# Positive parts on ScalarE, masked keys from PSUM, half-block masks on VectorE, and a new order in a two-layer attention kernel

## The chip, the cores and the metric

The kernel runs on one core of a Trainium2 chip. Four engines compute: TensorE (PE in the profile; its weight loads are listed apart as PEld), VectorE (DVE), ScalarE (ACT) and GpSimd (POOL). SyncE (SP) issues transfers only. Each engine works through its own queue in order, and they wait for each other by semaphores. The metric is the device time of one execution in microseconds (us); of several runs the median is taken.

## The reference

One sequence of 2048 tokens with 512 features passes through four blocks, each a residual: linear attention (A), sliding-window attention (B), A, B. There are 32 heads of 16 features.

```python
def _A_ref(x, wqkv, wo):            # linear attention
    ...
    phi = lambda t: jnp.where(t > 0, t + 1, jnp.exp(t)) + 1e-6
    pq, pk = phi(q), phi(k)
    kv = jnp.einsum("bhsd,bhse->bhde", pk, v)
    z = jnp.einsum("bhsd->bhd", pk)
    num = jnp.einsum("bhqd,bhde->bhqe", pq, kv)
    den = jnp.einsum("bhqd,bhd->bhq", pq, z)[..., None] + 1e-6
    o = num / den
    ...
def _B_ref(x, wqkv, wo):            # attention over a window of W = 256
    ...
    scores = jnp.einsum("bhqd,bhkd->bhqk", q, k) * (Dh ** -0.5)
    mask = (idx[:, None] - idx[None, :] >= 0) & (idx[:, None] - idx[None, :] < W)
    scores = jnp.where(mask[None, None], scores, -1e9)
    p = _softmax(scores, axis=-1)
    o = jnp.einsum("bhqk,bhkd->bhqd", p, v)
    ...
x = A_x
x = x + _A_ref(_layernorm(x, axis=-1), A_wqkv, A_wo)
x = x + _B_ref(_layernorm(x, axis=-1), B_wqkv, B_wo)
x = x + _A_ref(_layernorm(x, axis=-1), A_wqkv, A_wo)
x = x + _B_ref(_layernorm(x, axis=-1), B_wqkv, B_wo)
```

## The kernel before

**Tiles and phases.** The 2048 tokens are 16 tiles of 128, and x stays on the chip (`xres`). The first linear attention needs a sum over all tokens before any query can be answered, so `graph` (line 929) first runs `a_kv` for all 16 tiles (names beginning "1."): normalization, key and value projection, feature map of the keys, and the sum `kv`. Then comes the first `segment` ("2."): `a_q` and `a_out` per tile finish the first A block, `b_qkv` ("2.b.") makes queries, keys and values of the first B block, and `b_attn` ("2.a.") attends over the window. In the prediction this B block is called layer one and the second one layer two; the title of the change calls the half-block masks those of "layer two", since that block is the second of the four. Keys and values of the second A block ("2k.") follow tile by tile as tiles come out of the first B block, and after their sum the second segment ("3.", "3.b.", "3.a.") does the same as the first and writes the output.

**The feature map.** exp(t) is at most 1 for t <= 0, so phi(t) = max(t, 0) + min(exp(t), 1) + 1e-6. `phi` (lines 677 to 682) takes an exponential on ACT from PSUM (line 679), a minimum and addition on DVE in SBUF (680), and on DVE a maximum with zero of the PSUM bank plus the rest (681). The bank is free after line 681.

**Masked keys.** Scores are taken for four heads at once in four row groups of 32 rows, each of which holds two heads of 16. So that one head's key doesn't meet the other head's query, the keys are stored twice, each time with the rows of one head set to zero: `kbd`. Before, the key bank is copied to `kT` (by ACT or DVE, line 649), and then DVE multiplies `kT` by the two columns of the 0/1 mask `mab` (line 767).

**A tile's attention.** A query tile of 128 tokens needs five blocks of 64 keys that are partly or wholly visible per half: four blocks in "full" scores (`s0` to `s3`, one for each group of eight heads, line 840) and two half blocks (`sH`, lines 803 and 810). In the half blocks, the masked positions get a large negative addend by extra matmuls on PE with the constants `key` and `far` (line 810); then ACT takes the exponentials (830). In the full blocks ACT takes the exponentials first (847) and DVE multiplies two 64-column blocks by the triangles `tri` (859). Value products (871 and 883) sum values and row sums in PSUM, DVE divides (893 and 895), and `wo` (684) transposes the result, projects it and adds it to `xres` (689). Transposes are a DMA of SP (632), or, where the tile is listed in `BYPE`, four PE transposes (639) with a copy out of PSUM (649).

**The order.** Nothing in the code above fixes when an operation runs. `ORDER` (line 304) lists all 2630 operations by the number under which the code creates them. An apostrophe behind a number picks the second engine of those the operation may run on (ACT first, DVE second, for the copies). `schedule` places operations in that order, gives them a free buffer of their ring or a free bank of the eight of PSUM (some operations take two), and `emit` writes each engine's queue in the same order with the needed waits. Costs such as `_act_cost`, `tail` and `kind` are the planner's own figures and don't change what an instruction does. Each engine's queue is therefore the list, with the other engines' entries left out, and what an operation waits for follows from its reads, its writes and from who last held its buffer.

Of the kernel before, what the change touches and what calls it, by code (L numbers as in the profile page):

```python
# [320 lines left out]
909 452 453 454 868 1346 1347 1348 1349 659 660 875 910 911 642 677 661 884 885 455 1350 886 887 662 629 630 631 663 633 634 614 635 888 889 890 891 913 892
893 894 895 678 643 896 897 644 645 914 915 916 968 441 442 443 969 636 444 970 695 905 632 906 907 637 638' 456 942 943 603 908 944 1351 679 457 458 912 898
899 900 680 646 901 1360 1361 1362 1363 917 921 918 647 648 649' 919 696 946 947 948 922 651 652 653 920 926 927 1001 923 1002 1003 713 1338 1339 650 949 1340
924 925 928 929 930 931 1364 938 939 945 1357 1341 1342 940 941 1352 1353 1354 1355 604 1356 654 655 656 975 976 977 1358 1359' 954 955 681 956 957 958 664
950 951 932 933 934 1374 952 953 1365 1375 1376 682 665 666 667 979 1377 980 1378 981 1379 669 670 671 959 960 978 1034 1035 1036 961 962 963 964 1371 982 971
972 973 672 673 1372 1008 1009 1010 674' 1373' 974 1366 1367 987 1368 1369 1370 988 983 639 640 984 965 966 683 684 697 1011 668 698 985 685 986 989 699 700
967 1012 1013 1014 990 992 993 994 991 1067 1068 690 691 995 996 687 1390 1391 1069 1392 1004 1005 692' 657 714 715 686 688 689' 1385 1386 1387' 1041 716 1006
1007 997 998 999 658 717 1042 675 676 1000 1043 1044 1020 1016 1017 1018 1021 1022 1023 1024 1015 705 1019 1045 1046 1393 1394 1047 701 702 703' 1025 1026
1027 1028 1029 1100 1380 1404 1405 704 1101 1102 1381 1395 1406 1407 708 1408 1382 1383 709 706 1037 1048 459 460 710 711 1401 1402 1038 707' 1384 461 462 463
1039 1030 1040 1074 1075 1076 464 465 466 467 468 1053 712 1403' 1054 1055 1056 1057 1049 1050 1051 1031 1032 1033 1078 1079 1080 1052 718 1077 719 720 721'  # L330
722 1058 1133 1134 1135 469 1418 1419 470 1059 1060 1061 1070 1071 471 1072 1062 1063 723 724 472 725' 1073 1107 1108 693 1396 1397 731 732 733 734 735 1109
736 1086 1087 1398 1399 1082 1400 1083 1084 1064 1065 726 727 728 729 1088 1111 1112 1113 1081 1085 1091 1066 1092 1089 1090 1093 1094 1095 1096 1114 1166
# [56 lines left out]
class _Kernel:  # L389
# [238 lines left out]
    def transp(self, n, src, ring, dma=True):  # L628
        s = self.s
        o = ring.buf()  # L630
        if dma:
            s.op(n, {"SP": 1.25}, lambda e, en: e.dma_start_transpose(o.h[:], src.h[:]), reads=[src], writes=[o], new=[o], dma=True)
            return o
# [396 lines left out]
```

## Time and profile before

| | us |
|---|---|
| median of 3 runs | 446.47 |
| lowest and highest run | 443.78, 449.55 |
| the profiled execution, whole | 444.76 |
| its span, first to last instruction | 443.5 |

The mean TensorE clock of the profiled execution was 0.992 of full speed. A line of the profile's groups names source line, engine, operation, output <- input with partitions x elements, a count, then busy us and the mean ns of one, then the idle time before them and what ended it. The view of windows gives an engine's busy time in a stretch of the span, and the chain of waits follows the work that ended last backwards through whatever released it.

### The profile page before, as it was taken

What the parts mean: (1) busy time and instruction counts of PE and PEld (TensorE: products, weight loads), DVE (VectorE), ACT (ScalarE), POOL (GpSimd) and SP (SyncE); (2) the same over time, 40 slices, a digit from 0 to 9 for tenths busy, and PEclk for the clock granted to TensorE, in tenths of its full rate; (3) what the DMA queues carried; (4) which work ended last, traced back from release to release, by engine and by line L of the source; (5) the groups of instructions that cost most, each with busy time, mean ns of one, the idle gap of its engine ahead of it and who ended that gap; (6) DMA issues with size and microseconds to landing.
All of it is one profiled execution on the core that took longest, in us unless ns stands there. A gap on an engine that the chain in (4) does not pass through costs nothing.

```text
span 443.5 us, 19469 instructions
## 1 busy us (share of the span) xinstructions
PE 397.8 (90%) x8641; PEld 283.1 (64%) x8725; DVE 356.4 (80%) x947; ACT 362.4 (82%) x466; POOL 119.3 (27%) x248
## 2 busy tenths in 40 slices
PE   7989798898999998999899989999888898898886
PEld 3535676566666676667586577686666677675554
DVE  7998898899778788789877899899788876665545
ACT  3746236899999999899988545889898999999993
POOL 5428234132123403021304003143153105204100
PEclk9999999999999999999999999999999999999969
DMA  8691334334142213222323002253263212404323
GB/s 271 173 217 29 43 76 72 51 69 62 27 72 42 60 39 56 41 52 51 62 41 60 15 13 51 38 88 68 40 80 72 44 29 59 72 15 71 98 39 98
DMA packets 76660, 29.46 MB, mean 66 GB/s; under 512 B 66336, under 2 KB 74528, under 8 KB 76576
## 3 DMA queue, kind: packets, MB, share of 16 engines
q1 hardware_dynamic: 70896, 22.17, 26.5%
q0 software_dynamic: 4096, 4.46, 4.8%
q10 hardware_dynamic: 1584, 1.57, 1.1%
q8 instruction: 69, 1.13, 1.1%
q14 instruction: 15, 0.12, 0.1%
HBM read 6.29 MB, written 2.10 MB: 19 GB/s over the span
## 4 chain that ended last, share of the span: by engine, by line
ACT 36%; PE 33%; DVE 20%; DMA 7%; issue 2%; POOL 1%; SPq 0%
ACT pF L847 27%; PE ps L658 11%; PE ps L670 7%; ACT pH L830 7%; PE ps L883 5%; DVE stats L618 3%; PE ps L840 3%; PE ps L871 3%; DMA oT<-o 3%; DVE pq L681 3%; DVE o L749 2%; DMA xT<-xn 2%; DVE xres L689 2%; DVE xn L624 1%; PE ps L803 1%
## 5 line engine op out<-in xcount | busy, mean ns | idle before, releaser
L847 ACT ACTIVATE pF<-ps 128x1024 bf16<-128x1024 f32 (+2 forms) x256 | 230.7, 1016 | 9.3 <-PE ps L840 8.3
L622 POOL TENSOR_TENSOR rstd<-mv,const 128x1 f32<-128x1 f32 x64 | 37.0, 581 | 211.5 <-DVE mv L621 211.4
L778 POOL DMA_DIRECT2D vbd<-vt x128 | 67.5, 534 | 80.0 <-DVE vt L649 53.1
L859 DVE TENSOR_TENSOR pF<-pF,const 128x512 bf16<-128x512 bf16 (+1 forms) x128 | 50.1, 399 | 19.3 <-ACT pF L847 18.8
L830 ACT ACTIVATE pH<-ps 128x1024 bf16<-128x1024 f32 (+1 forms) x64 | 59.2, 989 | 6.5 <-PE ps L810 6.2
L679 ACT ACTIVATE E<-ps 128x512 bf16<-128x512 f32 x64 | 38.5, 607 | 29.0 <-PE ps L670 18.5
L883 PE MATMUL ps<-vbd,pF 128*128 128x34 bf16 x1920 | 61.2, 178 | 0.1
L840 PE MATMUL ps<-qT,kbd 32*128 32x128 bf16 x1920 | 50.3, 218 | 9.4 <-ACT pF L847 5.1
L883 PEld LDWEIGHTS ps<-vbd,pF 128*128 128x128 bf16 x1920 | 55.2, 96 | 3.8 <-issue 0.2
L689 DVE TENSOR_TENSOR xres<-ps,xres 128x512 bf16<-128x512 f32 x64 | 43.9, 686 | 13.9 <-PE ps L658 13.2
L840 PEld LDWEIGHTS ps<-qT,kbd 32*128 32x128 bf16 x1920 | 28.8, 93 | 34.2 <-ACT pF L847 18.6
L618 DVE BATCH_NORM_STATS2 stats<-xres 128x6 f32<-128x512 bf16 x64 | 43.8, 686 | 1.2 <-DMA xres<-in_A_x_dram 0.4
L670 PE MATMUL ps<-xT,w_Bk 128*128 128x128 bf16 x512 | 34.1, 219 | 2.9 <-DMA xT<-xn 2.2
L871 PEld LDWEIGHTS ps<-vbd,pH 128*128 128x128 bf16 x960 | 29.9, 96 | 10.6 <-issue 3.3
L871 PE MATMUL ps<-vbd,pH 128*128 128x34 bf16 x960 | 34.8, 179 | 1.2 <-DVE pF L859 0.4
L658 PE MATMUL ps<-w_Bo,oT 128*128 128x512 bf16 x105 | 29.3, 387 | 6.9 <-issue 1.9
L670 PE MATMUL ps<-xT,w_Bq 128*128 128x128 bf16 x512 | 34.9, 219 | 0.1
L670 PEld LDWEIGHTS ps<-xT,w_Bk 128*128 128x128 bf16 x512 | 29.7, 98 | 7.2 <-DMA xT<-xn 3.0
L658 PE MATMUL ps<-w_Av,xTa 128*128 128x512 bf16 x120 | 31.8, 379 | 2.6 <-DMA xTa<-xn 0.8
L670 PE MATMUL ps<-xTa,w_Aq 128*128 128x128 bf16 x512 | 34.0, 219 | 0.0
L658 PE MATMUL ps<-w_Ak,xTa 128*128 128x512 bf16 x119 | 31.3, 380 | 3.0 <-DMA xTa<-xn 1.4
L658 PE MATMUL ps<-w_Ao,oT 128*128 128x512 bf16 x102 | 27.8, 379 | 6.3 <-issue 3.1
(78 smaller groups left out, 563.4 us busy)
## 6 DMA issues: line engine op xcount, KB each, us to landing
vbd<-vt POOLq DMA_DIRECT2D x128, 34.0 KB, 2.0
xres<-in_A_x_dram SPq DMA_DIRECT2D x16, 128.0 KB, 6.1
out_dram<-xres SPq DMA_DIRECT2D x16, 128.0 KB, 2.1
oT<-o SPq DMA_TRANSPOSE x61, 2.7
w_Ak<-in_A_wqkv_dram ACTq DMA_DIRECT2D x1, 512.0 KB, 4.5
w_Av<-in_A_wqkv_dram ACTq DMA_DIRECT2D x1, 512.0 KB, 6.2
w_Aq<-in_A_wqkv_dram ACTq DMA_DIRECT2D x1, 512.0 KB, 8.6
w_Ao<-in_A_wo_dram SPq DMA_DIRECT2D x1, 512.0 KB, 6.7
```

Of the source, the lines that this page charges most:

```text
L618: s.op(n + ".st", {"DVE": 0.595}, lambda e, en: e.bn_stats(a_st, x.h[:]), reads=[x], writes=[st])
L658: i = e.matmul(g.h, xT.h[:, kt, :], w.h[:, kt, :], start=(kt == 0), stop=(kt == 3), skip_group_check=True)
L670: i = e.matmul(g.h[:, f * P:(f + 1) * P], w.h[:, kt, f * P:(f + 1) * P], xT.h[:, kt, :], start=(f == 0 and kt == 0), stop=(kt == 3), skip_ ...
L679: s.op(n + ".e", {"ACT": _act_cost(512)}, lambda e, en: e.activation(E.h[:], g.h, ACT.Exp, bias=0.0), reads=[g], writes=[E])
L689: s.op(n + ".x", {"DVE": _dve_cost(512)}, lambda e, en: e.tensor_tensor(x.h[:], g.h, x.h[:], ALU.add), reads=[g], writes=[x])
L778: return [e.dma_start(vbd.h[64 * a:64 * a + 64, j, a], vt.h[64 * j:64 * j + 64, a]) for j in range(2)]
L830: return e.activation(d, c, ACT.Exp, bias=0.0, scale=DH ** -0.5)
L840: i = e.matmul(ss[r // 2].h[:, r % 2, m * P:m * P + P], kbds[fj[m] // 2].h[32 * r:32 * r + 32, f, fj[m] % 2, :], qT.h[32 * r:32 * r + 32, ...
L847: s.op("e%d%d" % (f, g), {"ACT": _act_cost(2 * (4 - m0) * P)}, lambda e, en, S=ss[g], pb=pb, g=g: e.activation(pb.h[:, 2 * g:2 * g + 2, m0 ...
L859: return e.tensor_tensor(v, v, tr, ALU.mult)
L871: i = e.matmul(U.h[:, c:c + 34], pH.h[:, 4 * r + f, 64 * a:64 * a + P], vbds[j // 2].h[:, j % 2, :, 4 * f + r, :], start=first[0], stop=Tr ...
L883: i = e.matmul(U.h[:, c:c + 34], pFs[f].h[:, r, m * P:m * P + P], vbds[fj[m] // 2].h[:, fj[m] % 2, :, 4 * f + r, :], start=False, stop=Tru ...
```

## The change

1. `PHIA` names three of the four groups of feature maps (keys of the first A block, queries of both; 16 each). There, ACT also takes a Relu of the bank straight into the result, and DVE adds the other part from SBUF.
2. The ring `kT` is gone. Two operations `kb0` and `kb1` a tile write the two halves of `kbd` straight from the PSUM bank, each on ACT (a copy with the mask column as its scale) or on DVE.
3. In the first B block the extra matmuls with `key` and `far` are left out for the half blocks, and two DVE multiplications `mH0` and `mH1` a tile apply the triangles to the exponentials.
4. Tile 0 of the first B block and of the A block before it are transposed on PE (`BYPE`).
5. The last tile of the second B block masks its full blocks by extra matmuls on PE, and ends in `b_end`: four groups of eight heads, each with its own value products, division, transpose, copy and part of the output product; the residual addition and the output transfer run in two halves.
6. `ORDER` is new from its first line to its last, 2732 entries. The copies of queries, values and normalized tiles change engine in places with it.

The diff without the numbers of the order:

```diff
-BYPE = {("x1.", t) for t in range(6)} | {("a2.", 15), ("k2.", 15), ("o3.", 0), ("x3.", 0), ("a3.", 15)}
+PHIA = ("1.k","2.q","3.q")
+HMD = ("2.a.",)
+BYPE = {("x1.", t) for t in range(6)} | {("a2.", 15), ("k2.", 15), ("o3.", 0), ("x3.", 0), ("a3.", 15)} | {("o2.",0),("x2.",0)}
...
-            self.r_kT = self.ring("kT", 3, [P, 4, P])
...
-            s.op(n, {"SP": 1.25}, lambda e, en: e.dma_start_transpose(o.h[:], src.h[:]), reads=[src], writes=[o], new=[o], dma=True)
+            s.op(n, {"SP": 1.25}, lambda e, en: e.dma_start_transpose(o.h[:], src.h[:]), reads=[src], writes=[o], new=[o], dma=True,
+                 tail=1.0 if s.at[0] == "1." else 0.0)
...
+        if s.at[0] + n in PHIA:
+            s.op(n + ".r", {"ACT": _act_cost(512)}, lambda e, en: e.activation(view(o), g.h, ACT.Relu), reads=[g], writes=[o])
+            s.op(n + ".a", {"DVE": 0.335}, lambda e, en: e.tensor_tensor(view(o), view(o), E.h[:], ALU.add), reads=[E], writes=[o])
+            return
...
-        gk = self.proj_feat("k", xT, self.w["Bk"], kT, kbd)
-        self.copy("kc", kT, gk, lambda: (kT.h[:].rearrange("p f c -> p (f c)"), gk.h))
...
-        s.op("kb", {"DVE": 0.525}, kb, reads=[kT, self.mab], writes=[kbd])
+        gk = self.proj_feat("k", xT, self.w["Bk"], kbd)
+        for a in range(2):
+            def kb(e, en, a=a):
+                o = kbd.h[:, :, :, a * 64:a * 64 + 64].rearrange("p f j c -> p (f j) c")
+                g, m = gk.h.rearrange("p (b c) -> p b c", c=64), self.mab.h[:, a:a + 1]
+                return e.activation(o, g, ACT.Copy, scale=m) if en == "ACT" else e.tensor_scalar(o, g, m, None, op0=ALU.mult)
+
+            s.op("kb%d" % a, {"ACT": _act_cost(512), "DVE": _dve_cost(512)}, kb, reads=[gk, self.mab], part=[kbd])
...
-            for a, j in pcs:
+            for a, j in () if s.at[0] in HMD else pcs:
...
-            s.op("eH%d" % g, {"ACT": _act_cost(512 * len(pcs))}, ex, reads=[ss[g]], part=[pH])
+            mH = mH + [_Buf()]
+            s.op("eH%d" % g, {"ACT": _act_cost(512 * len(pcs))}, ex, reads=[ss[g]], writes=[mH[g]], part=[pH])
+        for g in range(2) if s.at[0] in HMD else ():
+            def mkH(e, en, g=g):
+                v = vH(g)
+                tr = self.tri.h[:].unsqueeze(1).to_broadcast([P, 8, 2, 64]) if len(pcs) == 2 else self.tri.h[:, 1:2, :].to_broadcast([P, 8, 64])
+                return e.tensor_tensor(v, v, tr, ALU.mult)
+
+            s.op("mH%d" % g, {"DVE": 0.065 + 0.00054 * 512 * len(pcs)}, mkH, reads=[self.tri, mH[g]], part=[pH])
...
+                for ty, h in ((0, 0), (0, 1), (3, 0), (3, 1)) if split else ():
+                    for r in range(4):
+                        c = ss[r // 2].h[:, r % 2, (64 if ty == 0 else 384) + 32 * h:][:, 0:32]
+                        k = self.key.h[32 * r:32 * r + 32, (0 if ty == 0 else 2) + h].rearrange("p a h c -> p (a h c)")
+                        i = e.matmul(c, k, self.far.h[32 * r:32 * r + 32, ty // 3, 0, :], start=False, stop=True,
+                                     skip_group_check=True, tile_position=(32 * r, 0))
...
+            if split:
+                continue
             s.op("m%d" % f, {"DVE": 0.34 if m0 == 0 else 0.2}, mask, reads=[self.tri], writes=[pb])
+        if split:
+            return self.b_end(t, o, pH, pFs, pcs, fj, vbds, w)
...
+    def b_end(self, t, o, pH, pFs, pcs, fj, vbds, w):
...
+        ys = [self.pG.buf(), self.pG.buf()]
+        for f in range(4):
...
+            s.op("z%dh" % f, {"PE": 0.0255 * 4 * len(pcs)}, pvH, reads=[pH] + [vbds[j // 2] for _, j in pcs], writes=[U], new=[U], kind="sum")
...
+                s.op("z%d%d" % (f, hf), {"PE": 0.0252 * 8}, pvF, reads=[pFs[f]] + [vbds[j // 2] for j in fj], writes=[U], kind="sum")
...
+            s.op("zr%d" % f, {"DVE": 0.12}, lambda e, en, uv=uv, dn=dn: e.reciprocal(dn.h[:, 0:8].unsqueeze(2), uv()[:, :, 16:17]),
+                 reads=[U], writes=[dn], new=[dn], tail=0.11)
+            s.op("zm%d" % f, {"DVE": 0.2}, lambda e, en, f=f, uv=uv, dn=dn: e.tensor_tensor(
+                o.h[:, f * P:f * P + P].rearrange("p (h e) -> p h e", e=DH), uv()[:, :, 0:16],
+                dn.h[:, 0:8].unsqueeze(2).to_broadcast([P, 8, DH]), ALU.mult), reads=[U, dn], part=[o], new=[o] if f == 0 else [])
+            s.op("zT%d" % f, {"PE": 0.1}, lambda e, en, f=f, tp=tp: e.transpose(tp.h.bitcast(BF)[:, 0:P], o.h[:, f * P:f * P + P], self.ident.h[:]),
+                 reads=[o, self.ident], writes=[tp], new=[tp, oT])
...
+            for c in range(2):
+                s.op("zw%d%d" % (f, c), {"PE": 0.12}, lambda e, en, f=f, c=c, oT=oT: e.matmul(
+                    ys[c].h[:, 0:256], oT.h[:, 0, :], w.h[:, f, 256 * c:256 * c + 256], start=(f == 0), stop=(f == 3), skip_group_check=True),
+                    reads=[oT, w], writes=[ys[c]], new=[ys[c]] if f == 0 else [], tail=0.1, kind="tok")
+        for c in range(2):
+            hx = _Buf()
+            s.op("zx%d" % c, {"DVE": _dve_cost(256)}, lambda e, en, c=c: e.tensor_tensor(
+                x.h[:, 256 * c:256 * c + 256], ys[c].h[:, 0:256], x.h[:, 256 * c:256 * c + 256], ALU.add), reads=[x, ys[c]], writes=[hx])
+            d = s.op("zo%d" % c, {"SP": 0.45}, lambda e, en, c=c: e.dma_start(
+                self.out[0, t * P:(t + 1) * P, 256 * c:256 * c + 256], x.h[:, 256 * c:256 * c + 256]), reads=[hx], dma=True)
...
```

More of the change, by code (lines that the diff above doesn't have):

```diff
@@ L321 @@
[L321 to L332, printed above, removed]
@@ new lines @@
+495 1123 1124 761 518 519 757 506 522 496 497 498 1471 1472 1161 1120 1467 1125 758 520 521 1468 1162 1163 762' 759' 1191 1134 1138 1139 1140 1135 1136 1469'
+1165 1166 1155 499 500 501 1164 1137 1143 1141 1142 1222 1473 1167 502 765 766 767 1223 768 1224 1225 1113 1114 1115 1157 1158 1159 1144 769 1145 770 1196
+1197 1198 1146 1147 1462 1463 1464 523 1160 1168 1173 1174 1116 1474 1475 508 1175 1176 1169 1170 1171 1488 1177 771 772 1465 773 774 509 1466 510 1148 511
+1489 512 775 513 778 779 776 1200 1172 1178 1179 1180 746 780 1201 1498 777' 1181 1182 1257 1202 1203 763 1149 1150 1151 1258 1259 1514 1515 1495 1192 1193
@@ L759, in b_qkv @@
         kbd, qT, vbd = self.r_kbd.buf(), self.r_qT.buf(), self.r_vbd.buf()
-        kT, vt = self.r_kT.buf(), self.r_vt.buf()
-        gk = self.proj_feat("k", xT, self.w["Bk"], kT, kbd)
-        self.copy("kc", kT, gk, lambda: (kT.h[:].rearrange("p f c -> p (f c)"), gk.h))
-        def kb(e, en):
-            src = kT.h[:].rearrange("p f (j c) -> p f j c", j=2)
-            for a in range(2):
-                i = e.tensor_scalar(kbd.h[:, :, :, a * 64:a * 64 + 64], src, self.mab.h[:, a:a + 1], None, op0=ALU.mult)
-            return i
-        s.op("kb", {"DVE": 0.525}, kb, reads=[kT, self.mab], writes=[kbd])
+        vt = self.r_vt.buf()
+        gk = self.proj_feat("k", xT, self.w["Bk"], kbd)
[5 more added lines that the diff above has]
+            s.op("kb%d" % a, {"ACT": _act_cost(512), "DVE": _dve_cost(512)}, kb, reads=[gk, self.mab], part=[kbd])
         gq = self.proj_feat("q", xT, self.w["Bq"], qT)
@@ L786, in b_attn @@
         m0 = {0: 3, 1: 1}.get(t, 0)
+        split = last and t == self.T - 1
         fj = [2 * t - 3 + m for m in range(4)]
@@ L813, in mmH @@
             return i
-        ss = scores("sH", pH, [j for _, j in pcs], mmH, 0.24 * len(pcs) + 0.02)
+        ss = scores("sH", pH, [j for _, j in pcs], mmH, 0.24 * len(pcs) + 0.02 - (0.115 * len(pcs) if s.at[0] in HMD else 0))
         def vH(g):
@@ L820, in vH @@
             return d if len(pcs) == 2 else d[:, :, 1, :]
+        mH = []
         for g in range(2):
@@ L842, in mmF @@
                                      skip_group_check=True, tile_position=(32 * r, 0))
+                for ty, h in ((0, 0), (0, 1), (3, 0), (3, 1)) if split else ():
[4 more added lines that the diff above has]
+                                     skip_group_check=True, tile_position=(32 * r, 0))
                 return i
-            ss = scores("s%d" % f, pb, fj[m0:], mmF, 0.025 + 0.056 * (4 - m0))
+            ss = scores("s%d" % f, pb, fj[m0:], mmF, 0.025 + 0.056 * (4 - m0) + (0.09 if split else 0))
             for g in range(2):
@@ L898, in b_attn, with pvH, pvF, uv @@
         self.wo("o", o, w, t, last, dma)
+    def b_end(self, t, o, pH, pFs, pcs, fj, vbds, w):
+        s = self.s
+        x = self.xres[t]
+        ys = [self.pG.buf(), self.pG.buf()]
+        for f in range(4):
+            U, dn, tp, oT = self.pG.buf(), self.r_dn.buf(), self.pG.buf(), self.r_oT.buf()
+            def pvH(e, en, f=f, U=U):
+                for r in range(4):
+                    for a, j in pcs:
+                        i = e.matmul(U.h[:, r * 34:r * 34 + 34], pH.h[:, 4 * r + f, 64 * a:64 * a + P], vbds[j // 2].h[:, j % 2, :, 4 * f + r, :],
+                                     start=(r == 0 and j == pcs[0][1]), stop=True, skip_group_check=True)
+                return i
+            s.op("z%dh" % f, {"PE": 0.0255 * 4 * len(pcs)}, pvH, reads=[pH] + [vbds[j // 2] for _, j in pcs], writes=[U], new=[U], kind="sum")
+            for hf in range(2):
+                def pvF(e, en, f=f, U=U, hf=hf):
+                    for r in (2 * hf, 2 * hf + 1):
+                        for m in range(4):
+                            i = e.matmul(U.h[:, r * 34:r * 34 + 34], pFs[f].h[:, r, m * P:m * P + P], vbds[fj[m] // 2].h[:, fj[m] % 2, :, 4 * f + r, :],
+                                         start=False, stop=True, skip_group_check=True)
+                    return i
+                s.op("z%d%d" % (f, hf), {"PE": 0.0252 * 8}, pvF, reads=[pFs[f]] + [vbds[j // 2] for j in fj], writes=[U], kind="sum")
+            def uv(U=U):
+                return U.h[:, 0:136].rearrange("p (h e) -> p h e", e=17)
+            s.op("zr%d" % f, {"DVE": 0.12}, lambda e, en, uv=uv, dn=dn: e.reciprocal(dn.h[:, 0:8].unsqueeze(2), uv()[:, :, 16:17]),
[5 more added lines that the diff above has]
+                 reads=[o, self.ident], writes=[tp], new=[tp, oT])
+            self.s.op("zc%d" % f, {"ACT": _act_cost(P), "DVE": _dve_cost(P)}, lambda e, en, oT=oT, tp=tp: e.activation(
+                oT.h[:, 0, :], tp.h.bitcast(BF)[:, 0:P], ACT.Copy) if en == "ACT" else e.tensor_copy(oT.h[:, 0, :], tp.h.bitcast(BF)[:, 0:P]),
+                reads=[tp], writes=[oT])
+            for c in range(2):
[8 more added lines that the diff above has]
+                self.out[0, t * P:(t + 1) * P, 256 * c:256 * c + 256], x.h[:, 256 * c:256 * c + 256]), reads=[hx], dma=True)
+            d.final = True
+            d.signals = True
```

70 lines of the change are left out of this document (40 added, 30 removed), and 73 rows, old and new, of the table ORDER.

## The prediction

> **What bounds the kernel now.** First the page's head and its shares of busy time: no engine is a clear bound.
>
> ```profile
> span 443.5 us, 19469 instructions
> PE 397.8 (90%) x8641; PEld 283.1 (64%) x8725; DVE 356.4 (80%) x947; ACT 362.4 (82%) x466; POOL 119.3 (27%) x248
> ACT 36%; PE 33%; DVE 20%; DMA 7%; issue 2%; POOL 1%; SPq 0%
> ```
>
> The third line is the chain that ended last: it passes from ScalarE (ACT) to TensorE (PE) to VectorE (DVE), a third each, so shares over the whole span decide nothing. I therefore cut the span into eight stages and asked the view of windows for the busy time in each. The cuts are the starts of a tile's half-block exponentials (pH, line 830) or the end of a layer's last exponential: layer one tiles 0, 4, 12 and its end, then layer two tiles 0, 4 and its end. Columns: stretch, length, then busy us and instructions of PE, PEld, DVE, ACT, POOL, the clock, DMA.
>
> ```profile
> 0.00:71.40 71.40, 62.59 (x550) 37.22 (x558) 63.21 (x181) 32.64 (x56) 32.79 (x86) 1.00 0.53 131
> 71.40:96.30 24.90, 23.34 (x542) 17.03 (x544) 21.39 (x59) 21.66 (x37) 7.37 (x14) 1.00 0.35 58
> 96.30:183.20 86.90, 79.86 (x2035) 57.51 (x2054) 70.68 (x186) 83.54 (x98) 21.56 (x40) 1.00 0.30 51
> 183.20:241.10 57.90, 53.87 (x1235) 38.06 (x1247) 47.73 (x127) 54.63 (x65) 14.61 (x27) 1.00 0.30 54
> 241.10:273.90 32.80, 31.28 (x449) 23.63 (x451) 30.20 (x80) 16.86 (x31) 2.62 (x5) 1.00 0.11 22
> 273.90:318.30 44.40, 41.17 (x872) 31.16 (x882) 39.58 (x111) 38.05 (x59) 12.51 (x24) 1.00 0.36 61
> 318.30:436.20 117.90, 102.03 (x2907) 76.43 (x2932) 80.59 (x205) 114.39 (x126) 27.82 (x53) 0.97 0.31 59
> 436.20:443.50 7.30, 3.62 (x62) 2.07 (x60) 3.04 (x7) 0.60 (x1) 0.00 (x0) 0.96 0.32 92
> ```
>
> The reader is to see three regimes. Stages 3, 4 and 7 (263 us) belong to ScalarE at 96, 94 and 97% busy. Stages 1 and 5 belong to PE and DVE together, with ScalarE under half busy (32.64 of 71.4 and 16.86 of 32.8). Stages 2 and 6 have all three at 85 to 94%. Work given to ScalarE is cheap in stages 1 and 5 and dear in 3, 4 and 7.
>
> **The prices.** An instruction that queues behind another of its engine costs less than its own duration, so I take the step from one to the next out of the chain and the timeline (start, us, engine, line, count).
>
> ```profile
> 380.07 7.33 ACT pF L847 x8
> 33.46 4.26 PE ps L658 x19
> 250.47 1.08 ACT L649 ACTIVATE vA<-ps 128x512 bf16<-128x512 f32 x2
> 263.12 1.28 DVE L681 SCALAR_TENSOR_TENSOR pq<-ps,E 128x512 bf16<-128x512 f32 x2
> 98.11 0.75 DVE L859 TENSOR_TENSOR pF<-pF,const 128x512 bf16<-128x512 bf16 x2
> 272.21 0.60 DVE L767 TENSOR_SCALAR kbd<-kT,const 128x512 bf16<-128x512 bf16 x2
> 272.73 0.68 DVE L681 SCALAR_TENSOR_TENSOR pq<-ps,E 128x512 bf16<-128x512 f32 x1
> 75.18 0.41 PE L810 MATMUL ps<-const 32*128 32x128 bf16 x16
> 75.53 0.68 PE L670 MATMUL ps<-xT,w_Bk 128*128 128x128 bf16 x9
> L859 DVE TENSOR_TENSOR pF<-pF,const 128x512 bf16<-128x512 bf16 x112 | 45.9, 415 | 17.9 <-ACT pF L847 17.4
> L859 DVE TENSOR_TENSOR pF<-pF,const 128x256 bf16<-128x256 bf16 x16 | 4.2, 286 | 1.4 <-ACT pF L847 1.4
> L679 ACT ACTIVATE E<-ps 128x512 bf16<-128x512 f32 x64 | 38.5, 607 | 29.0 <-PE ps L670 18.5 <-PE ps L658 10.2
> ```
>
> - ACT: 1024 columns 7.33/8 = 0.92 us; 512 columns 1.08 - 0.60 = 0.48.
> - DVE: 512 columns from PSUM 1.28 - 0.68 = 0.60; 512 from SBUF 0.75 - 0.415 = 0.34; a kb pair 272.73 - 272.21 = 0.52. A 1024-column multiply: 415 + 2 x (415 - 286) = 673 ns, less the same 0.08 of overlap, 0.59.
> - PE: 512 columns 4.26/19 = 0.224, so half a projection 0.45; a tile's 16 half-block mask matmuls 75.53 - 75.18 = 0.35 at most.
>
> **Part by part.**
> (1) Positive part. Each of 48 maps gets a Relu on ACT (+48 x 0.48 = 23.0) and its DVE step becomes an SBUF addition in place of a PSUM one (-48 x 0.26 = -12.5). No Relu is in this trace. From below it is an ACT copy out of PSUM (0.48), from above a lone one (0.607); I take 0.48, since it queues behind its own exponential. Exponentials behind it in ScalarE's queue wait those 0.48 longer; the addition waits for it.
> (2) Masked keys. Before: a copy (17 on ACT, 15 on DVE) and a DVE pair. After: 64 half writes from PSUM, 19 on ACT and 45 on DVE by the apostrophes in the new order; eight query copies and other copies move too. ACT: -17 + 19 - 8 + 1 copies, -5 x 0.48. DVE: -15 x 0.60 - 32 x 0.52 + 45 x 0.60 + 7 x 0.60 = +5.6. A half write from PSUM isn't in the trace; between the SBUF half (0.26) and the PSUM copy (0.60) I take 0.60, its source being PSUM. The key bank is now held until both writes end; the two steps in a row become two that may run side by side.
> (3) Layer-one (the code's "2.a.") half-block masks: PE loses at most 16 x 0.35 = 5.6; DVE gains 28 x 0.59 + 4 x 0.34 = 17.9. What waits for them is the first half-block value product, queued behind four score groups; DVE's queue waits behind each mask for its exponential.
> (4) Two more tile-0 transposes on PE with a copy on ACT, in place of SP's DMA, at the start of layer one.
> (5) The tail, below. The dropped key ring frees memory alone; the 1.0 on a transpose is the planner's figure; POOL (27% busy) keeps its statistics and moves in number, and SP issues two transposes less.
>
> In all ACT gains some 22 us and DVE some 10, PE loses about 3: the change adds work. It can only win by where the new order puts it. I named the numbers of both orders, cut them at the same events, and priced the differences. Half projections are h.
>
> 1. Before layer one's first scores: ACT +26 Relus; DVE -10 (23 lighter additions; two fewer residual additions, one fewer statistics, two fewer normalizations); PE -8 h, +2 transposes, -1 numerator pair: -3.0. PE bound: **-3.0**. PE idles 8.8 us here, and DVE, its equal so far, falls to 53; the two transposes leave a queue that shows up as
>
> ```profile
> 47.90 8.65 SPq L632 DMA_TRANSPOSE oT<-o  x5
> 63.26 4.77 DMA xT<-xn
> 5.60 0.60 PE L639 MATMUL ps<-const,xn 128*128 128x128 bf16 x4 [0.32 <-DVE xn L624]
> ```
>
>    1.73 us each in the queue and 4.77 on the chain against 0.60 and a copy of 0.60. I take **-2.0** more; the ends are 0 and -5.
> 2. ACT +0.4, DVE +1.1, PE -1.0: **+0.5**.
> 3. Four Relus and half writes against fewer copies: ACT **+2.0**. DVE takes 17 of the masks, +13.1, and goes from 70.68 to 83.8 of 88.9 us: 81% to 94%.
> 4. Work is brought forward into this stage (two more key maps of the next layer, four of its query maps): ACT **+6.8**, DVE +8.0, PE +5.6.
> 5. In return PE -2.5, DVE -4.0 (ACT +3.5, from 16.86): **-2.5**.
> 6. PE -9.4 (18 h and smaller pieces moved to stages 3 to 5 and 7), DVE -3.5, ACT -3.9. The bound goes from PE's 41.17 to DVE's 36.1: **-5.1**.
> 7. ACT unchanged (112.3 by my prices in both orders), DVE +6.2, PE +8.1 to 110 of 117.9: **0**.
> 8. The tail:
>
> ```profile
> 436.16 0.42 DVE L859 TENSOR_TENSOR pF<-pF,const 128x512 bf16<-128x512 bf16 x1 [0.29 <-ACT pF L847]
> 437.06 0.96 PE L883 MATMUL ps<-vbd,pF 128*128 128x34 bf16 x32
> 438.35 0.42 DVE L895 TENSOR_TENSOR o<-ps,dn 128x256 bf16<-128x256 f32 x1
> 439.26 0.60 ACT L649 ACTIVATE oT<-ps 128x512 bf16<-128x512 bf16 x1 [3.14 <-PE ps L639]
> 440.00 1.02 PE L658 MATMUL ps<-w_Bo,oT 128*128 128x512 bf16 x4 [0.78 <-ACT oT L649]
> 441.07 0.69 DVE L689 TENSOR_TENSOR xres<-ps,xres 128x512 bf16<-128x512 f32 x1 [1.45 <-PE ps L658]
> ```
>
>    With four groups the mask (0.42) and its wait are gone from DVE, the value products are 0.5 in place of 1.0, the copy 0.25 for 0.60, the output product 0.25 for 1.02, and the addition 0.35 a half: 2.9 less, against two additions and two output transfers in turn, 0.8 more. **-2.1.** The masks go to PE, which idles in stage 7.
>
> Beside these, stage 3 brings DVE to 94% beside ACT at 96%. Stage 6 of before shows three near-equal engines: the busiest reaches 41.17/44.4 = 93%, not the 96% of stage 3. Between nothing and stage 3 at that ratio (85.5/0.93 - 88.9 = 3) I take **+1.0**.
> Sum: -3.0 - 2.0 + 0.5 + 2.0 + 6.8 - 2.5 - 5.1 + 0 - 2.1 + 1.0 = **-4.4**, 443.5 to 439.1 us of span. The profiled execution took 444.76 (1.26 beside the span), which makes 440.4; the median of the three runs, 446.47, lies 1.7 above it, so **442 us**.
>
> The Trainium skill ("ScalarE: Activation LUTs", What ACT_TABLE_LOAD costs) gives about 93 ns more to an ACTIVATE for each pointer operand of one value a partition. The new key writes on ACT have one as their scale, and no run here shows it. Fourteen of the 19 stand in stages 2 to 4, 6 and 7, so by the page the sum would be some 1.3 us higher, an estimate.
>
> **Rivals.**
> - *The order closes idle time* (0.34). The busiest engine's idle is 8.2 us in stage 1, 3.2 in stage 6, 3.3 in stage 4 and 3.5 in stage 7. If DVE's relief and the earlier key writes take 3, 3, 1.5 and 2.5 of these beyond my terms, 10 go: 432 us. For it: DVE has 10 us less in stage 1. Against: it has more in 3, 4 and 7.
> - *VectorE's half-block masks take over the path* (0.10, slower). In stages 3 and 4 the DVE queue gets 26 masks, 15.3 us. If each is met by an empty ring of pF, the softmax masks behind it start late, value products hold their PSUM banks, and scores and ACT wait: 442 + 15.3 = 457. It makes the kernel slower by 2% only if 13.3 of the 15.3 lie on the path. Against: DVE has 16.2 and 10.2 us free there.
> - *Relu is the wrong work for ScalarE* (0.03, slower). My sum charges Relus as ScalarE's only where ScalarE bounds; the 35 in stages 1 and 5 ride free. If each delayed its map by its 0.48, 17 us: 459. Against: ACT is idle 39 and 16 us there, and on PSUM sources it steps faster (0.48) than DVE (0.60). The Trainium skill (same page, Rules for kernel authors) says relu belongs on VectorE, up to about three times faster in bf16; the rows just named disagree for a float32 source in PSUM.
> - *Relu costs table loads* (0.01): one each way, 96 of the 1.28 below, 123 us: 565. Against: copies and exponentials alternate all through with two loads in all.
>
> ```profile
> L649 ACT ACT_TABLE_LOAD x1 | 1.3, 1283 | 2.4 <-issue 2.4
> L943 ACT ACT_TABLE_LOAD x1 | 1.3, 1283 | 0.0
> ```
>
> **How the numbers follow.** My forecast has 0.52 and a range of its own of 437 to 450: the ends of stage 1's term, the 3 us of stage 3, a lone Relu's price. A measurement of this kernel tells about 2% from no change (437.5 and 455.4). So faster 0.34 (first rival), same 0.52, slower 0.14 (the others). The range 430 to 453 leaves out the far part of the first rival (0.06) and most of the slower ones (0.12).
>
> **What would show it.** Stage by stage: the first half-block exponential at about 66 us, not 71.4; layer one's last exponential some 5 us later than 241; layer two's tile 0 near 276 to 279; its last exponential near 434; 5.2 us after that. ACT busy near 384, DVE near 366, and the half-block mask line on DVE near 0.6 us a piece. I am wrong if stage 1 isn't shorter, if stage 3 grows by over 6, or if ScalarE waits in stage 7.

## The result and the profile after

The changed kernel takes 432.47 us (median of 4 runs, 430.78 to 433.92) against 445.92 (4 runs) for the kernel before: a ratio of 0.9689, interval 0.9615 to 0.9763. It is 3% faster. The forecast was 442 in a range of 430 to 453, with "no change" as the likeliest case: the range holds the time, the likeliest case was the wrong one, and the time is the one that the rival "the order closes idle time" was priced at (432). How far that rival's mechanism is what happened is taken up below. Of the 9.5 us between 442 and the result, 6.4 lie in the span (439.1 forecast, 432.7 measured); the rest is the step from the profiled execution to the median, +1.7 in the forecast and -1.5 here (433.92 to 432.47). The profiled execution has this span and these shares:

```profile
span 432.7 us, 19801 instructions
PE 408.5 (94%) x8801; PEld 286.6 (66%) x8801; DVE 367.9 (85%) x954; ACT 383.3 (89%) x513; POOL 121.8 (28%) x248
PE 38%; ACT 35%; DVE 17%; DMA 7%; issue 2%; POOL 1%; POOLq 0%; DVEq 0%
```

ACT is busy 383.3 us (forecast 384) and DVE 367.9 (forecast 366): the work did grow by some 21 and 11 us, and the span shrank by 10.8. The view of windows, cut at the same events as before (the pH exponentials of layer one's tiles 0, 4, 12, its last exponential, layer two's tiles 0 and 4, its last exponential), shows where:

```profile
0.00:64.20 64.20, 60.01 (x529) 35.83 (x529) 54.44 (x163) 44.81 (x83) 32.31 (x82) 1.00 0.48 124
64.20:90.90 26.70, 24.20 (x496) 16.37 (x497) 23.92 (x61) 22.21 (x36) 6.85 (x14) 1.00 0.42 80
90.90:181.00 90.10, 85.51 (x2149) 61.82 (x2148) 82.14 (x206) 87.36 (x105) 23.85 (x44) 1.00 0.33 55
181.00:243.00 62.00, 61.23 (x1352) 43.03 (x1350) 55.75 (x144) 60.52 (x77) 15.17 (x28) 1.00 0.30 52
243.00:273.10 30.10, 29.48 (x389) 21.53 (x388) 27.68 (x78) 19.88 (x39) 4.76 (x9) 1.00 0.13 26
273.10:307.80 34.70, 32.68 (x728) 23.43 (x727) 31.12 (x83) 33.01 (x50) 10.86 (x21) 1.00 0.34 62
307.80:427.50 119.70, 112.95 (x3144) 83.35 (x3141) 90.69 (x218) 114.77 (x127) 27.96 (x53) 1.00 0.34 59
427.50:432.70 5.20, 2.42 (x29) 1.25 (x28) 2.14 (x7) 0.76 (x4) 0.00 (x0) 1.00 0.55 180
```

The clock (last column but two) was 1.00 in stages 1 to 6 before and after, and 0.97 and 0.96 before in stages 7 and 8 only, so it doesn't explain what stages 1 to 6 gained or lost.

TensorE's busy time must not be compared between these two profiles as it stands. The profile before has 8641 matmuls for 8725 weight loads: 84 matmuls of the 512-column projections (L658) left no record. The one above has all 8801. The run e5 below is the same changed kernel again, and its profile lacks 84 of them too, as the one before does:

```profile
PE 396.1 (92%) x8717; PEld 286.0 (66%) x8801; DVE 368.0 (85%) x954; ACT 383.3 (89%) x513; POOL 121.8 (28%) x248
0.00:64.04 64.04, 58.16 (x523) 35.18 (x529) 54.47 (x163) 44.82 (x83) 32.36 (x82) 1.00 0.48 125
64.04:90.67 26.63, 23.34 (x491) 16.30 (x497) 23.89 (x61) 22.27 (x37) 6.82 (x14) 1.00 0.45 78
90.67:180.14 89.47, 82.94 (x2128) 61.85 (x2148) 81.97 (x206) 87.26 (x105) 23.86 (x44) 1.00 0.33 55
180.14:242.23 62.09, 59.43 (x1338) 43.01 (x1350) 55.80 (x144) 60.55 (x77) 15.18 (x28) 1.00 0.30 51
242.23:272.26 30.03, 29.14 (x384) 21.55 (x388) 27.66 (x78) 19.82 (x38) 4.71 (x9) 1.00 0.13 26
272.26:307.00 34.74, 32.04 (x722) 23.40 (x727) 31.12 (x83) 33.05 (x49) 10.93 (x21) 1.00 0.34 61
307.00:426.30 119.30, 108.65 (x3117) 83.42 (x3141) 90.93 (x218) 114.82 (x127) 27.96 (x53) 1.00 0.34 59
426.30:431.50 5.20, 2.38 (x29) 1.25 (x28) 2.10 (x7) 0.72 (x3) 0.00 (x0) 1.00 0.55 180
```

TensorE's busy time differs by 12.4 us between the two profiles of the same kernel (408.5 and 396.1), about 0.15 us a record, while the other engines agree within 0.1 us and the stages within 0.7. So the table takes the lengths from both and the rest from e5. For each stage, take its busiest engine out of e5's lines and out of the table before the change; what is left of the stage is time in which even that engine has nothing on record.

| stage | forecast | measured | in e5 | e5: busiest engine's work | its idle time, before -> e5 |
|---|---|---|---|---|---|
| 1 to first exponential | -5.0 | -7.2 | -7.4 | -5.0 | 8.2 -> 5.9 |
| 2 layer one, tiles 0-4 | +0.5 | +1.8 | +1.7 | +0.6 | 1.6 -> 2.7 |
| 3 tiles 4-12 | +3.0 | +3.2 | +2.6 | +3.7 | 3.4 -> 2.2 |
| 4 to its end | +6.8 | +4.1 | +4.2 | +5.9 | 3.3 -> 1.5 |
| 5 between the layers | -2.5 | -2.7 | -2.8 | -2.1 | 1.5 -> 0.9 |
| 6 layer two, tiles 0-4 | -5.1 | -9.7 | -9.7 | -8.1 | 3.2 -> 1.7 |
| 7 to the last exponential | 0 | +1.8 | +1.4 | +0.4 | 3.5 -> 4.5 |
| 8 tail | -2.1 | -2.1 | -2.1 | -1.2 | 3.7 -> 2.8 |

The busiest engines' work fell by 5.9 us in all (415.2 to 409.3) and their idle time by 6.1 (28.3 to 22.2). The forecast had -3.4 for the work and -1.0 for the idle time.

One part did not do what it says. Below, the groups of the changed kernel and of the one before in the stretch 60 to 245 us, which is layer one, and then the DVE multiplication of the changed kernel:

```profile
L818 PE MATMUL ps<-const 32*128 32x128 bf16 x240 | 6.2, 215 | 0.0
L810 PE MATMUL ps<-const 32*128 32x128 bf16 x240 | 6.3, 215 | 0.0
L847 DVE TENSOR_TENSOR pH<-pH,const x32: 391/682/691, 65.6 to 238.2; 128x1024 bf16<-128x1024 bf16 x28, 128x512 bf16<-128x512 bf16 x4
```

All 240 masking matmuls of layer one are still there. The line `for a, j in () if s.at[0] in HMD else pcs` stands in a function that runs when the queues are written out, and by then `s.at` holds the name of the last phase built, "3.a.", whatever tile the function belongs to. The two loops over `mH` and the positive parts ask at the time of building and do work. So the changed kernel masks layer one's half blocks twice, on TensorE before the exponential and on VectorE behind it (a zero times zero). The description in "The change", item 3, is what the code means to do, not what runs.

### The profile page after: what moved, and what is told of

The parts are those of the page before. It is cut to its first block, busy times and chain, and to the rows that moved or that the text cites. A ratio compares the mean times of both kernels' runs of the same rounds, so it can differ in the third digit from the quotient of the medians.

```text
span 432.7 us, 19801 instructions
## 1 busy us (share of the span) xinstructions
PE 408.5 (94%) x8801; PEld 286.6 (66%) x8801; DVE 367.9 (85%) x954; ACT 383.3 (89%) x513; POOL 121.8 (28%) x248
## 4 chain that ended last, share of the span: by engine, by line
PE 38%; ACT 35%; DVE 17%; DMA 7%; issue 2%; POOL 1%; POOLq 0%; DVEq 0%
ACT pF L870 24%; PE ps L663 14%; PE ps L675 7%; ACT pH L839 7%; PE ps L910 4%; DMA oT<-o 4%; PE ps L857 4%; PE ps L898 2%; DVE stats L622 2%; DVE o L758 2%; DVE xres L698 2%; ACT E L684 2%; DVE xn L628 1%; DVE kbd L775 1%; PE ps L720 1%
## 5 line engine op out<-in xcount | busy, mean ns | idle before, releaser
L910 PEld LDWEIGHTS ps<-vbd,pF 128*128 128x128 bf16 x1856 | 54.1, 96 | 5.4
L882 DVE TENSOR_TENSOR pF<-pF,const 128x512 bf16<-128x512 bf16 (+1 forms) x124 | 47.5, 398 | 9.8 <-ACT pF L870 9.5
L698 DVE TENSOR_TENSOR xres<-ps,xres 128x512 bf16<-128x512 f32 x63 | 42.9, 683 | 6.4 <-PE ps L663 6.3
L675 PE MATMUL ps<-xT,w_Bk 128*128 128x128 bf16 x512 | 35.1, 219 | 2.0 <-DMA xT<-xn 1.6
L675 PE MATMUL ps<-xT,w_Bq 128*128 128x128 bf16 x512 | 36.1, 219 | 0.8 <-issue 0.4
L775 DVE TENSOR_SCALAR kbd<-ps,const 128x512 bf16<-128x512 f32 x45 | 31.9, 742 | 5.2 <-PE ps L675 4.7
L663 PE MATMUL ps<-w_Ao,oT 128*128 128x512 bf16 x128 | 33.7, 380 | 1.4 <-DMA oT<-o 0.9
L663 PE MATMUL ps<-w_Ak,xTa 128*128 128x512 bf16 x128 | 33.8, 387 | 1.0 <-ACT xTa L654 0.8
L663 PE MATMUL ps<-w_Av,xTa 128*128 128x512 bf16 x128 | 34.6, 384 | 0.1
L675 PEld LDWEIGHTS ps<-xTa,w_Aq 128*128 128x128 bf16 x512 | 30.4, 98 | 6.4 <-issue 2.0
```

What stands on the lines that cost most here:

```text
L663: i = e.matmul(g.h, xT.h[:, kt, :], w.h[:, kt, :], start=(kt == 0), stop=(kt == 3), skip_group_check=True)
L675: i = e.matmul(g.h[:, f * P:(f + 1) * P], w.h[:, kt, f * P:(f + 1) * P], xT.h[:, kt, :], start=(f == 0 and kt == 0), stop=(kt == 3), skip_ ...
L698: s.op(n + ".x", {"DVE": _dve_cost(512)}, lambda e, en: e.tensor_tensor(x.h[:], g.h, x.h[:], ALU.add), reads=[g], writes=[x])
L882: return e.tensor_tensor(v, v, tr, ALU.mult)
L910: i = e.matmul(U.h[:, c:c + 34], pFs[f].h[:, r, m * P:m * P + P], vbds[fj[m] // 2].h[:, fj[m] % 2, :, 4 * f + r, :], start=False, stop=Tru ...
```

## The experiments

All twelve were timed in five rounds beside the kernel before. They fall into three sittings, on two chips, in which the kernel before took 444.39 us (e1 to e4), 444.87 (e5 to e8) and 446.14 (e9 to e12); so a difference between runs of two sittings is uncertain by a further 1 to 2 us. Orders were rewritten by name: an operation that an edit adds or drops is put in or taken out at the place named below, and where no PSUM banks or ring buffers were free any more, a few entries were moved later. The expectations name three theories: A, the order carries the gain and the parts only make it possible; B, relieving VectorE where ScalarE is idle carries it, whatever the order; C, the order alone carries it.

**The base again.**

> The changed kernel once more, so that the runs beside it have their base on the same chip: 431 to 434 us, ratio near 0.969.

433.16 us (0.974, interval 0.9704 to 0.9777), first half-block exponential at 64.04 us, span 431.5. The differences below are taken against this.

**Layer one's masks.**

```diff
-HMD = ("2.a.",)
+HMD = ()
```

> The changed kernel with layer one's half-block masks back on TensorE, the order otherwise the same. If the masks on VectorE cost what the prediction put in (about 1 us net): 430.5 to 432.5. If TensorE (95 and 99% busy in stages 3 and 4 of the changed kernel) is what bounds there: 16 x 0.35 = 5.6 us of work comes back, 435 to 438.

433.94 us (0.9765, 0.9743 to 0.9786), between the two times on record. Since TensorE's masks had never gone, this run doesn't move them: it only drops the 32 multiplications from VectorE, whose busy time fell to 352.0 us. It tells less than it was meant to, but one thing clearly: 16 us of VectorE's time, most of it in stages 3 and 4 at 91 and 90% busy, were worth nothing (433.94 against 433.16, intervals overlapping). These multiplications don't bound there. TensorE's 95 and 99% in the expectation come from the profile with all records; e5's has 93 and 96%. Whether TensorE without its 240 matmuls would make those stages shorter was not tried, and stays open.

**The positive part.**

```diff
-PHIA = ("1.k","2.q","3.q")
+PHIA = ("2.q","3.q")          # e8; () in e3
...
 order: "<map>.r" taken out, "<map>.a" replaced by "<map>.p" right behind the later of ".r" and ".m"
```

> The changed kernel with the positive part back on VectorE for the 16 key maps of the first stage alone. By the prediction's bound (TensorE, with at most half of its idle time lent by VectorE) 0 to 2 us: 432 to 435. If each map's VectorE time lies on the path of the first stage, as the run without any Relu suggests (10.7 us for 26 maps there): 16/26 of it, 6 to 7 us, 438 to 440, all of it before the first half-block exponential (64.2 us).

436.77 us (0.9823, 0.9793 to 0.9854), 3.6 above the base. The first half-block exponential of this run and of the base:

```profile
68.11 1.08 ACT L839 ACTIVATE pH<-ps 128x512 bf16<-128x512 f32 x2 [0.21 <-PE ps L818]
64.04 1.08 ACT L839 ACTIVATE pH<-ps 128x512 bf16<-128x512 f32 x2 [0.41 <-issue]
```

It starts 4.1 us later, and from there to the end of the span the two run alike (367.2 and 367.5 us). That is 16 x 0.26 = 4.2, the whole price of the heavier VectorE step, and VectorE's busy time in the stage grew by as much (54.47 to 58.72 us). TensorE now waits for that step (L690), 3.0 us in stage 1, where it waited 0.5 for the lighter one of the same maps (L688) in the base:

```profile
PE ps L720 <- DVE pk L690: 1.3, 2, 1.0
PE ps L663 <- DVE pk L690: 0.9, 1, 0.9
PE ps L644 <- DVE pk L690: 0.8, 1, 0.8
```

So in stage 1 VectorE's time lies on the path. The result falls between the two numbers on record: more than the 0 to 2 of a TensorE bound, less than the 6 to 7 read off e3.

> The changed kernel with the 48 positive parts back on VectorE, each maximum as soon as the bank's exponential and minimum are through. If the relief of VectorE is the main cause (A and B alike): 438 us or more, with the first stage (to the first half-block exponential) at 67 us or more where it is 64.2, and layer two's start (tiles 0 to 4, now 34.7 us) longer by 2 or more. If Relu brings nothing: 431 to 434.

470.37 us (1.0583, 1.0556 to 1.061). Both signs that the expectation names for VectorE's relief are there: the first half-block exponential at 74.95 us, and layer two's start 37.7 us long for 34.7. But 37 us is three times the 48 x 0.26 = 12.5 that the Relus took from VectorE. Dozens of other entries of the order had to move to find banks, and ScalarE, with 19 us less to do than in the changed kernel (364.5), waited 34 us for scores. The granted clock was lower too (0.985, base 1.00), and the same 8717 recorded matmuls took 404.2 us for 396.1. This run can't be read as the price of the Relus.

**The masked keys.**

```diff
-            s.op("kb%d" % a, {"ACT": ..., "DVE": ...}, kb, reads=[gk, self.mab], part=[kbd])
+        self.copy("kc", kT, gk, ...)                                  # at the first half write's place
+        s.op("kb", {"DVE": 0.525}, kb, reads=[kT, self.mab], writes=[kbd])   # at the second's; e11: two DVE entries later
```

> The changed kernel with the masked keys in two steps again: a copy of the bank at the place of the first half write (on ScalarE where one of the two halves was there), the DVE pair at the place of the second. By work alone nothing changes (a copy and 0.52 us for two half writes): 431.5 to 434. If the shorter way from the bank to the masked keys is what closed idle time: 437 us or more, most of it in layer two's start (34.7 us) and in layer one's tiles.

451.6 us (1.0157, 1.0117 to 1.0198): 18.4 us more than the base, with the same work (ACT 380.3, DVE 368.6 us busy). VectorE stood 9.0 us before copies that ScalarE hadn't done, which could be my placing; hence the next run.

> The run e6_two_step_keys once more with the DVE pair two VectorE instructions later in the order, so that VectorE seldom stands before a key copy that isn't through (9.0 us of waiting in that run). If that wait made the 18.5 us: 442 or less. If the longer way from bank to masked keys made it, through scores and exponentials that start late: 447 or more.

446.24 us (1.0003, 0.9976 to 1.003). The wait at VectorE's head fell to 4.6 us and the time by 5.4 (the two runs are of two sittings). 13.1 us remain, so neither bound that was on record was met: about a third was the place, the rest the longer way itself or what else the order has fitted to the short one. What carries it is ScalarE's wait for scores. The view of ScalarE's waits, for the run e11 and then for the base:

```profile
ACT pH L843 <- PE ps L822: 12.9, 13, 2.9
ACT pF L874 <- PE ps L861: 12.2, 29, 0.8
...
ACT pF L870 <- PE ps L857: 5.9, 16, 0.8
ACT pH L839 <- PE ps L818: 4.1, 9, 0.8
```

25.1 us against 10.0: 15 us of waiting, 13 us of time. A tile's scores can't start before its keys are masked, and ScalarE, which is the busiest engine in stages 3, 4, 6 and 7, has then nothing to take.

**The tail.**

```diff
-        split = last and t == self.T - 1
+        split = False
```

> The changed kernel with the last tile as before (masks on VectorE, two groups, one transpose, one output product, one transfer). The prediction gave the four groups 2.1 us: 2 to 3 us slower than the changed kernel, 434 to 436, and from the last exponential to the end 7.3 us in place of 5.2. A rival: the last stage is ended by the two transfers, then under 1 us slower.

446.64 us (1.0032, 1.0005 to 1.006). The operations of the old ending stood where the new groups had stood; TensorE met value products whose masks weren't through and held the next scores back, and ScalarE waited up to 3.6 us for the last tile's scores. It shows the place, not the ending.

> The changed kernel with the last tile as before, its operations standing between the last tile's scores and exponentials as in the old order (the run e7_old_tail had put value products ahead of scores in TensorE's queue, and exponentials waited up to 3.6 us). If the four groups bring what the prediction gave them: 2 to 3 us slower than the changed kernel, 434.5 to 436.5.

438.58 us (0.9819, 0.9791 to 0.9848): 5.4 more than the base, where 2 to 3 were on record. The last exponential ends at 427.57 us of the span, where the changed kernel's ends at 427.54, so the runs differ behind it alone: 9.5 us to the end against 5.2, a difference of 4.3; in the old order the same ending took 7.3. Not all of the 4.3 is the ending's own. The clock behind the last exponential was 0.70 in this profile, against 0.96 before and 1.00 in the changed kernel, and the output product's matmuls took longer; here are the window of e12 and its group, then the group before:

```profile
427.57:437.10 9.53, 4.47 (x74) 2.70 (x73) 2.99 (x7) 0.60 (x1) 0.00 (x0) 0.70 0.25 85
L663 PE MATMUL ps<-w_Bo,oT 128*128 128x512 bf16 x6 | 2.3, 504 | 1.2 <-ACT oT L654 1.1
L658 PE MATMUL ps<-w_Bo,oT 128*128 128x512 bf16 x7 | 1.8, 377 | 0.8 <-ACT oT L649 0.8
```

Another part stands in VectorE's queue, tile 14's addition ahead of tile 15's last mask:

```profile
428.21 0.69 DVE L698 TENSOR_TENSOR xres<-ps,xres 128x512 bf16<-128x512 f32 x1 [1.68 <-PE ps L663]
428.81 0.41 DVE L882 TENSOR_TENSOR pF<-pF,const 128x512 bf16<-128x512 bf16 x1
429.70 0.96 PE L910 MATMUL ps<-vbd,pF 128*128 128x34 bf16 x32
433.18 1.48 PE L663 MATMUL ps<-w_Bo,oT 128*128 128x512 bf16 x3 [1.09 <-ACT oT L654]
434.70 0.69 DVE L698 TENSOR_TENSOR xres<-ps,xres 128x512 bf16<-128x512 f32 x1 [3.28 <-PE ps L663]
```

The last mask starts 1.2 us behind the last exponential, and the chain mask, products, division, transpose, copy, product, addition takes the rest. In the changed kernel it is shorter at each link:

```profile
427.59 0.57 PE L947 MATMUL ps<-vbd,pF 128*128 128x34 bf16 x16
428.20 0.21 DVE L956 RECIPROCAL dn<-ps 128x8 f32<-128x8 f32 x1 [0.41 <-PE ps L947]
428.51 0.29 DVE L958 TENSOR_TENSOR o<-ps,dn 128x128 bf16<-128x128 f32 x1
429.13 0.28 ACT L963 ACTIVATE oT<-ps 128x128 bf16<-128x128 bf16 x1 [0.59 <-PE ps L961]
429.78 0.76 DVE L972 TENSOR_TENSOR xres<-ps,xres 128x256 bf16<-128x256 f32 x2 [0.38 <-PE ps L967]
430.50 0.94 SPq L974 DMA_DIRECT2D out_dram<-xres  x2
```

**Parts without the order, order without the parts.**

```diff
 e1: all five parts; order: the old one, with
+  "<map>.r" behind "<map>.e", "mH" behind "eH"; "kc" -> "kb0", "kb" -> "kb1"; the tail as in the new order
 e2: none of the five parts; order: the new one, with
-  "<map>.r", "mH"; "kb0" -> "kc", "kb1" -> "kb"; the tail back in two groups
```

> All five parts of the change, put into the OLD order: each Relu directly behind its exponential, the first half key write where the copy stood and the second where the DVE pair stood, each half-block mask directly behind its exponential, the last tile's groups as in the new order. Theory A (the order carries the gain, the parts only make it possible): 444 us or more, because ScalarE gets 22 us and VectorE 10 us of work in the stages where they already bound. Theory B (VectorE's relief in the stages with an idle ScalarE carries the gain, whatever the order): 433 to 439 us.

501.48 us (1.1277, 1.1249 to 1.1305).

> The NEW order with all five parts undone (maximum on VectorE as soon as its two inputs stand, key copy at the first half write's place and the pair at the second's, masks on TensorE, old tail, transposes by DMA). Theory A would still need the parts: 440 us or more. A third theory, C (the order alone): within 2 us of the changed kernel, 431 to 435. Theory B: 444 to 448, as before the change.

492.58 us (1.1077, 1.1042 to 1.1111). The times that B and C forecast are far off, and neither the parts nor the order gained anything without the other as I placed them. A's bounds are met. But no theory is shown or refuted by this, since both mixtures are 48 to 57 us slower than the kernel before, though ACT (391.6 and 360.1 us busy) and DVE (368.8 and 368.5) have at most 9 us more to do than in the changed kernel. ScalarE waits 57.8 and 56.3 us for scores in them, against 14.5 before and 10.7 in the changed kernel:

```profile
ACT pF L847 <- PE ps L840: 8.3, 18, 1.5
ACT pH L830 <- PE ps L810: 6.2, 10, 1.1
ACT pF L870 <- PE ps L857: 6.0, 17, 0.6
ACT pH L839 <- PE ps L818: 4.7, 9, 0.8
```

In e1 VectorE also stands 23.1 us before the half-block multiplications, which I had put right behind their exponentials. In e2 the granted clock was 0.948, against 0.992 before, and the same 8641 recorded matmuls took 412.5 us for 397.8; so up to 15 of its 48 us may be the clock. What the two show is that an order is fitted to its own list of operations.

**Two attempts to beat both.**

```diff
-HMD = ("2.a.",)
+HMD = ()
 order, between "2.a.sH" of tile 4 and layer one's last exponential, same places:
-  9 half key writes on ACT                       (e10: and 10 copies; behind layer two's tile 4, 3 more)
+  the same with an apostrophe: on DVE
```

> A version meant to beat both: the changed kernel with layer one's half-block masks on TensorE (as in the run e4_masks_on_pe) and, in the room that this leaves on VectorE, the 9 half key writes that ScalarE does between layer one's tile 4 and its end moved to VectorE at the same places of the order. If ScalarE alone sets the pace there: 9 x 0.57 = 5 us less, 428 to 430. If the engines' queues are fitted to each other so closely that a moved instruction costs its neighbours a wait: no gain, 432 to 438.

438.81 us (0.985, 0.982 to 0.988).

> As e9_keys_to_dve, and also the 10 copies of queries and values that ScalarE does in that stretch and the 3 key and query copies that it does behind layer two's tile 4. ScalarE loses 22 x 0.48 to 0.57, some 11 us, in the stages that it bounds; VectorE gains 22 x 0.6 = 13 and gives 18 for the masks. ScalarE's pace alone: 422 to 427. Fitted queues: 432 to 440.

446.19 us (1.0013, 0.9989 to 1.0037). ScalarE's busy time did fall, to 378.9 and 373.9 us from 383.3, VectorE's stayed below the changed kernel's, and the time rose by 5.6 and 13.0 over e5 (4.9 and 12.3 over e4, from which they start). Both lie above even the range on record for fitted queues. ScalarE's waits for scores rose to 20.5 and 32.4 us, in e10:

```profile
ACT pF L870 <- PE ps L857: 21.6, 35, 2.0
ACT pH L839 <- PE ps L818: 10.8, 14, 1.6
```

No version beats the changed kernel.

## Why the prediction was right and where it failed

**Prices.** They held but for one. A Relu steps like an exponential:

```profile
257.59 0.60 ACT L684 ACTIVATE E<-ps 128x512 bf16<-128x512 f32 x1 [0.53 <-PE ps L675]
258.08 0.59 ACT L687 ACTIVATE pq<-ps 128x512 bf16<-128x512 f32 x1
L687 ACT ACTIVATE pk<-ps 128x512 bf16<-128x512 f32 x16 | 10.0, 631 | 2.2 <-PE ps L663 2.2
L688 DVE TENSOR_TENSOR pq<-pq,E 128x512 bf16<-128x512 bf16 x32 | 13.3, 417 | 0.9 <-ACT pq L687 0.3
L775 DVE TENSOR_SCALAR kbd<-ps,const 128x512 bf16<-128x512 f32 x45 | 31.9, 742 | 5.2 <-PE ps L675 4.7
L775 ACT ACTIVATE kbd<-ps,const 128x512 bf16<-128x512 f32 x19 | 12.6, 705 | 3.0 <-PE ps L675 2.9
L654 DVE CAST qT<-ps 128x512 bf16<-128x512 f32 x23 | 15.7, 685 | 5.1 <-PE ps L675 5.1
```

0.49 us from an exponential to its Relu (0.48 taken); the SBUF addition 417 ns beside the mask's 415 that it was priced by; the 1024-column multiplication 682 ns (673). The half write from PSUM costs VectorE 742 ns, some 55 more than a plain copy (685), so its step is nearer 0.66 than the 0.60 that I took, an estimate by the same 0.08 of overlap. The Relus brought no table load: there are two in all, as before.

**Stages 2, 3, 5 and 8** came out within 1.3 us: +1.8 for +0.5, +3.2 for +3.0, -2.7 for -2.5, -2.1 for -2.1. In stage 3 the agreement is luck: the work grew by 3.7 and not by 2.0, and the idle time fell where +1.0 was forecast. That +1.0 for near-equal engines rested on TensorE's 93% in stage 6 before, which is too low: about 10 of the stage's 882 matmuls left no record, and at 0.15 us each the share is some 96%, as in stage 3 (an estimate from the two profiles of the changed kernel). e4 shows that VectorE's 94% (91 measured) didn't matter. The tail's agreement is to the old ending in the old order; in the new order the old ending took 4.3 more, part of it at the lower clock (e12).

**Part 3** was priced for what it says, PE -5.6 and DVE +17.9. Only the second half happened, and it cost nothing. No rival of mine named that the edit might not take.

**Stage 6** is the step that failed most: "The bound goes from PE's 41.17 to DVE's 36.1: -5.1", and it went to ACT's 33.0, -9.7. I cut the order list at the same operations and counted what stood between them. VectorE's work in the stage fell by 8.5 us, not 3.5, and rose by 10.1 in stage 7, not 6.2, where it has room: together +1.6 for a counted +2.7. The sum over both was about right, the line between them wasn't. The likely reason is that a position in the list isn't a time, since another engine's queue may run ahead or behind there; no run tests that.

**Idle time** is the other step: I carried each stage's idle time over, less 2.0 in stage 1 and plus 1.0 in stage 3. It fell by 6.1 us: 2.3 in stage 1 (8.2 to 5.9), 1.7 in stage 4, 1.5 in stage 6, 1.2 in stage 3; in stage 7 it grew by 1.0. For stage 1 as a whole (-7.4 in e5), e8 shows the cause of 4 us: VectorE's time for the 16 key maps counts in full, where I let TensorE bound and lent VectorE 2.0; the value that I took lay inside my ends of 0 and -5 and should have been near the far one. The other 3 us (the ten query maps there, the half projections moved out, part 4's two transposes) were not separated. For stages 4 and 6, the direct keys are a likely cause (e6 and e11: with equal work, 13 to 18 us more time without them), but these runs change a way and its fit to the order together. How the idle time lost there divides between the parts and the new order stays open: the mixtures of parts and orders that I placed by hand lost more by misfit than what was to be measured. Of the recorded signs of being wrong, stage 1 is shorter and stage 3 grew by 3.2; ScalarE's idle time in stage 7 did grow, by 1.0 to 1.4 us.

**The rivals.** "The order closes idle time" has the right time and about half of the mechanism: it put 10 us of idle time beyond my terms, 2.5 of them in stage 7; some 5 went, and stage 7's grew. The rest came from work moved out of stage 6 and from the step to the median, so the meeting at 432 is partly luck. VectorE's masks on the path is refuted by e4: without them the time was the same (433.94 against 433.16), not 15.3 less. Relu as the wrong work for ScalarE is refuted by e8 for the 16 key maps of stage 1: giving them back to VectorE costs 3.6 us; no run settles it for the 32 query maps. The Trainium skill's advice to keep relu on VectorE ("ScalarE: Activation LUTs", Rules for kernel authors), whose figure is for bf16, doesn't hold for this float32 source in PSUM beside a ScalarE with room (44.8 of 64.0 us busy in stage 1). The same page's 93 ns for a pointer operand agrees: 705 ns for a key write with one against 609 to 631 for a Relu without.

## What to carry to other kernels

In this kernel, with three engines 85 to 94% busy, added work cost nothing (e4's 16 us on VectorE) and work taken off the busiest engine cost time (e10): look at what the pacing engine waits for (here ScalarE for scores: 14.5 us before, 10.7 after, 20 to 58 in the kernels that were slower through it), not at busy shares. A written-out order and its list of operations are one thing; an edit to either, judged without a new fit of the other, can measure mostly the misfit. And see that two profiles hold the same records before comparing busy times. Last, count an edit's instructions in the trace before explaining its effect: a condition inside a function that runs later may see another state than the one it was written for.

## What the runs showed of the hardware

A copy on ScalarE with a column of scales is about 80 ns dearer than without one (705 ns, against 608 to 644 for the plain copies out of PSUM), and a multiplication by a column on VectorE out of PSUM about 55 ns dearer than a plain copy (742 against 685 ns). I hadn't expected the second.
